# Second FFN planned like the first, unused matmuls at the beginning, other planned durations, norm powers in a stretch of their own

## The chip, the core and the metric

The kernel runs on one core of one Trainium2 chip. Its engines are TensorE (PE, with its weight loads listed apart as PEld), VectorE (DVE), ScalarE (ACT), GpSimd (POOL) and SyncE (SP), which here issues nearly all DMAs. Each engine works through its own queue in order. The metric is the device time of one execution in microseconds (us), the median over several runs. "Clock" is the TensorE clock that was granted, as a share of 2.4 GHz; its lower level is 1.2 GHz.

## The reference

Three steps follow each other: a gated linear attention (4 batches, 8 heads, 768 positions, 48 channels), and two feed-forward networks (FFNs) over 3072 tokens with 384 channels and 2048 hidden ones.

```python
mag = np.sqrt(a_re * a_re + a_im * a_im)
scale = np.minimum(mag, 0.999) / (mag + 1e-06)      # a_re, a_im are multiplied by it
for t in range(S):
    S_re, S_im = ar * S_re - ai * S_im + kv, ar * S_im + ai * S_re
    y[:, :, t] = np.einsum('bhd,bhde->bhe', q[:, :, t], S_re)
# first FFN: silu
h = x @ w_in;  g = h * (1.0 / (1.0 + np.exp(-h)));  x = g @ w_out
# second FFN, beta = 1
h = x @ w_in;  g = np.where(h >= beta, h, np.where(h <= -beta, 0.0, (h + beta) ** 2 / (4.0 * beta)));  out = g @ w_out
```

## The kernel before

**Tiling.** Attention is cut into 12 units (4 batches x 3 blocks of 256 positions). A unit squares a_re and a_im, makes the norm by a logarithm and an exponential (`power` or `window`), scans the decays in blocks (`scan`, nearly all VectorE), forms scaled q and k (`qprime`, `kprime`), transposes them on TensorE with copies by ScalarE (`trans`), and does scores, values and the running state on TensorE (`heads`, `state`). The first FFN goes over 6 pairs of units (512 tokens each) in 16 steps f: nine hidden matmuls into `ph` (`hidden`, L892 to L894), a gate (`gate`: Silu, high part gH, low part gL), and nine output matmuls into three accumulators (L913 to L915). Every product of an FFN is made of three matmuls, because operands are split into a high and a low part. Weights arrive as 64-bit numbers and are converted on VectorE, ScalarE and for some on TensorE (`convert`, 16 tiles for each FFN, k = 0 to 15 and 16 to 31). A tile of the second FFN's weights takes the buffer of one of the first, so its load waits for the last use of that.

**The plan.** `Plan` holds generators. Each yields an engine, a duration and an earliest time for its next operation, or the name of a mark or a ring slot it needs; `go` always takes the operation with the smallest start plus lag and emits it. The durations exist in the plan only: they decide the order of each engine's queue, and the hardware does the rest by semaphores. `lag` ranks the runs: units by their number, weights by `urgent`, the FFN by `behind` (FL = 0.2, or FB = 0.6 while it is ahead of attention).

**What is planned and what isn't.** `first_half` plans attention, the first FFN and all 32 conversions. Then comes a barrier, and the second FFN follows outside the plan, written in program order: `prep` loads one pair's x and splits it (L981, L983), `two` does 16 steps of hidden matmuls, gate (L1011 to L1016) and outputs (L998 to L1000), and the next pair's `prep` is emitted ahead of it. `flag_bad` (a check whether a slow path is needed) is emitted after the second pair.

**Norm powers.** For units 3 to 11 the norm's logarithm and exponential are done in `window` (L217) together with those of the unit before (SEP = 2): two logarithms, then two exponentials.

**Pair 0.** In the first FFN's pair 0 (PEL = 16) gL is made by a matmul with the negative identity (L933) and a copy (L935); in the other pairs by a subtraction on VectorE (L938).

Of the kernel before, what the change touches and what calls it, by code (L numbers as in the profile page):

```python
# [14 lines left out]
PAB = 2  # L15
# [8 lines left out]
class Plan:  # L24
# [6 lines left out]
    def __init__(self):  # L31
        self.free = dict.fromkeys((PE, DVE, ACT, SP, "DMA"), 0.0)
        self.at = {}
        self.runs = []
        self.table = "exp"
        self.log = []
        self.rings = {"t": [2], "pa": [PAB], "ph": [PHB], "gH": [3], "gL": [3], "xq": [1], "sc": [4]}
# [35 lines left out]
    def go(self):  # L73
        while self.runs:
# [30 lines left out]
class Attn:  # L105
# [35 lines left out]
    def loadq(self, i, c):  # L141
        x = self.U[i]["qk"[c]] = self.wp.tile([128, 768], F32, name="qk"[c] + "t")
        t = yield SP, 0.6, 0.0
# [3 lines left out]
    def loadv(self, i):  # L147
        nc, wp, U = self.nc, self.wp, self.U[i]
        U["v"] = []
        for c in range(2):  # L150
            U["v"].append(wp.tile([128, 8, 48], F32, name="vt", bufs=2))
            t = yield SP, 0.5, 0.0
# [88 lines left out]
    def scan(self, i, A, t0=0.0):  # L241
# [81 lines left out]
        if i:  # L323
            yield f"QT{i - 1}"
# [28 lines left out]
    def trans(self, src, nm, t0=0.0):  # L353
# [3 lines left out]
        for g0 in (0, 2):  # L357
# [9 lines left out]
            for g, ps, t1 in pend:  # L367
                t1 = yield ACT, 0.56, t1 + 0.2
# [17 lines left out]
    def knat(self, i):  # L386
        if i < EARLY:
            t0 = yield f"kT{i}"
            self.plan.mark(f"free{i}", t0)
            if i:  # L390
                yield f"st{i - 1}"
# [18 lines left out]
        if i:  # L410
            yield f"st{i - 1}"
# [8 lines left out]
        for c in range(2):  # L420
            kn = wp.tile([128, 8, 96], F32, name="KN", bufs=2)
            t1 = yield SP, 0.8, t2
# [7 lines left out]
    def scores(self, i, QT, KT, c, hh, AT, t0):  # L430
# [4 lines left out]
        t1 = yield PE, 0.95, t0  # L435
# [52 lines left out]
    def heads(self, i, QT, KT, vt, x, t0):  # L488
# [3 lines left out]
        hq, tq = yield "xq", 1  # L492
        xq = wp.tile([128, 2, 256], F32R, name="xq", bufs=1)
        for c in range(2):
            first = u == 0 and c == 0
            sc = []
            for hh in range(2):
                if c:
                    yield f"py{i}"
# [8 lines left out]
            t1 = yield PE, 1.0 + 1.0 * (not first), max(ta, tr, tf)  # L508
# [7 lines left out]
        if u < 2:  # L516
            yield from self.state(i, 1, vt)
        plan.mark(f"st{i}", 0.0)
# [29 lines left out]
    def unit(self, i, x):  # L548
# [36 lines left out]
        tk = yield f"k{i}"  # L585
        t1 = yield from self.kprime(A, U["k"], M[:, 1], r[:, 1], max(t1, tk))
        yield f"QT{i}"
        plan.mark(f"kp{i}", t1)
        if i:
            yield f"h{i - 1}"  # L590
# [4 lines left out]
        xi = yield from x(i)  # L595
        yield from self.heads(i, U["QT"], KT, U["v"], xi, max(t1, tv))

    def ahead(self, i):

        yield f"kp{i - 2}"  # L600
# [6 lines left out]
        t0 = yield f"A{i}"  # L607
# [7 lines left out]
    def queries(self, i, t0):  # L615
# [4 lines left out]
        if i:  # L620
            yield f"h{i - 1}"
# [8 lines left out]
def flag_bad(nc, pool, pp, at, ff):  # L630
    ok = pool.tile([128, 164], F32, name="ok")
    nc.vector.memset(ok, 1.0)
# [4 lines left out]
    low = pool.tile([128, 1], F32, name="low")  # L637
    nc.vector.tensor_reduce(low, ok, mybir.AxisListType.X, ALU.min)
    one = pool.tile([128, 1], F32, name="one")
    nc.vector.memset(one, 1.0)  # L640
    pf = pp.tile([128, 512], F32, name="pf", tag="pa", bufs=PAB)
    nc.tensor.matmul(pf[0:1, 0:1], low, one, start=True, stop=True)
    bad = pool.tile([1, 1], I32, name="bad")
    nc.vector.tensor_scalar(bad, pf[0:1, 0:1], 127.5, None, ALU.is_lt)
    return bad
# [153 lines left out]
class Ffn:  # L799
# [11 lines left out]
    def fetch(self, k):  # L811
        raw = self.wp.tile([128, 1536], I32, name="raw", tag=("wi", "wo")[k % 2] + str(k % 16 // 2))
        t = yield SP, 0.6, 0.0
# [83 lines left out]
    def one(self, n, x, dst):  # L897
        nc, wp, pp, plan = self.nc, self.wp, self.pp, self.plan
        acc = [pp.tile([128, 512], F32, name=f"acc{j}", tag=f"acc{j}") for j in range(3)]
        G = {}  # L900
# [3 lines left out]
        def outs(f):  # L904
            t0 = yield f"g{n}.{f}"
            if n == 0:
                t0 = max(t0, (yield f"w{f // 2 * 2 + 1}"))
            gH, gL, hH, hL = G.pop(f)
# [62 lines left out]
    def prep(self, src):  # L971

        nc, wp = self.nc, self.wp
        raw = wp.tile([128, 3, 512], F32, name="xraw", tag="A", bufs=2)
        x = wp.tile([128, 2, 3, 512], F32R, name="x", bufs=2)
        t = yield SP, 0.6, 0.0
        nc.sync.dma_start(raw, src.rearrange("(j p) t -> p j t", p=128))
        t = self.plan.dma(t, 786)
        for j in range(3):
            t1 = yield ACT, 0.56, t  # L980
            nc.scalar.copy(x[:, 0, j], raw[:, j])  # L981
            yield DVE, 0.61, t1
            nc.vector.tensor_tensor(x[:, 1, j], raw[:, j], x[:, 0, j], ALU.subtract)  # L983
        return x

    def two(self, x, out):
        xH, xL = x[:, 0], x[:, 1]
        nc, tc, wp, pp = self.nc, self.tc, self.wp, self.pp
        acc = [pp.tile([128, 512], F32, name=f"pacc{j}", tag=t, bufs=n)
               for j, (t, n) in enumerate((("acc0", 1), ("acc1", 1), ("acc2", 1), ("pa", PAB)))]  # L990
        pend = []

        def outs(f, gH, gL):
            oH, oL = self.wslices(f, 1)
            for t in range(4):
                s = slice(t * 128, (t + 1) * 128)
                o = acc[t][:, 0:384]
                nc.tensor.matmul(o, gH[:, s], oH, start=f == 0, stop=False)  # L998
# [3 lines left out]
        for f in range(16):  # L1002
            ph = pp.tile([128, 512], F32, name="ph", tag="ph", bufs=PHB)
            for _ in self.hidden(ph, f, xH, xL):
                pass
            c = wp.tile([128, 512], F32, name="c", tag="AT", bufs=2)
            l = wp.tile([128, 512], F32, name="l", tag="KN", bufs=2)
            g = wp.tile([128, 512], F32, name="g", tag="t", bufs=2)
            gH = wp.tile([128, 512], F32R, name="gH", bufs=3)
            gL = wp.tile([128, 512], F32R, name="gL", bufs=3)  # L1010
            nc.vector.tensor_scalar(c, ph, 1.0, -1.0, ALU.min, ALU.max)  # L1011
            nc.scalar.activation(l, ph, AF.Relu, bias=self.cst[:, 0:1])  # L1012
            nc.scalar.activation(c, c, AF.Square, bias=self.cst[:, 1:2], scale=0.5)  # L1013
            nc.vector.tensor_tensor(g, c, l, ALU.add)  # L1014
            nc.scalar.copy(gH, g)  # L1015
            nc.vector.tensor_tensor(gL, g, gH, ALU.subtract)  # L1016
            pend.append((f, gH, gL))
            if len(pend) > 1:
# [212 lines left out]
```

## Time and profile before

| | us |
|---|---|
| median of 3 runs (1159.58 to 1163.02) | 1161.08 |
| the profiled execution | 1160.27 |
| its span | 1158.6 |
| TensorE busy | 1028.6 (89%) |
| VectorE busy | 776.6 (67%) |
| ScalarE busy | 643.2 (56%) |

The span is the time from the first to the last instruction in the profile. Busy time of TensorE counts pipelined matmuls, so a busy TensorE can still run at a low clock: the granted clock has to be read beside it. Averages hide stages with different limits, so the rows below go by stretches: the start (up to 136 us), the first FFN coming in (136 to 204), attention and FFN side by side (204 to 640), the end of the first FFN (640 to 724), the step between the FFNs (724 to 755), and the second FFN (755 to 1128).

### The profile page before, as it was taken

What the parts mean: (1) busy time and instruction counts of PE and PEld (TensorE: products, weight loads), DVE (VectorE), ACT (ScalarE), POOL (GpSimd) and SP (SyncE); (2) the same over time, 40 slices, a digit from 0 to 9 for tenths busy, and PEclk for the clock granted to TensorE, in tenths of its full rate; (3) what the DMA queues carried; (4) which work ended last, traced back from release to release, by engine and by line L of the source; (5) the groups of instructions that cost most, each with busy time, mean ns of one, the idle gap of its engine ahead of it and who ended that gap; (6) DMA issues with size and microseconds to landing.
All of it is one profiled execution on the core that took longest, in us unless ns stands there. A gap on an engine that the chain in (4) does not pass through costs nothing.

```text
span 1158.6 us, 15058 instructions
## 1 busy us (share of the span) xinstructions
PE 1028.6 (89%) x5664; PEld 866.7 (75%) x5664; DVE 776.6 (67%) x1471; ACT 643.2 (56%) x1047; POOL 1.4 (0%) x16
## 2 busy tenths in 40 slices
PE   0374869999999999999999999399999999999997
PEld 0263658677877777787777888289989989989986
DVE  6878889687877877787787278654555355455443
ACT  4454496858385674838566356453555354445443
POOL 0000000000000000000000000000000000000000
PEclk9975879999999999999999999599999999999999
DMA  5402251233131323223221245500101000000000
GB/s 204 171 25 70 75 180 66 73 90 118 28 110 62 97 60 98 88 63 109 63 69 48 72 154 208 193 8 1 56 1 55 1 1 28 1 28 2 28 1 30
DMA packets 47280, 82.06 MB, mean 71 GB/s; under 512 B 24160, under 2 KB 32608, under 8 KB 47200
## 3 DMA queue, kind: packets, MB, share of 16 engines
q1 hardware_dynamic: 47056, 80.92, 21.1%
q8 instruction: 47, 0.77, 0.3%
q14 instruction: 33, 0.27, 0.1%
q10 hardware_dynamic: 144, 0.10, 0.0%
HBM read 61.34 MB, written 17.30 MB: 68 GB/s over the span
## 4 chain that ended last, share of the span: by engine, by line
PE 44%; ACT 4%; DVE 1%; DMA 1%; issue 1%; ACTq 0%; SPq 0%; DVEq 0%
PE ph L892 7%; PE ph L893 7%; PE ph L894 7%; PE pacc L999 6%; PE pacc L998 6%; PE pacc L1000 6%; PE acc L913 1%; PE acc L914 1%; PE acc L915 1%; DMA raw<-in_w_dram 1%; PE py L460 1%; PE psc L438 1%; ACT KT L369 1%; ACT r L217 0%; ACT L217 0%
## 5 line engine op out<-in xcount | busy, mean ns | idle before, releaser
L892 PE MATMUL ph<-x,wi 128*128 128x512 f32 x576 | 232.6, 404 | 17.3 <-ACT x L981 14.6
L893 PE MATMUL ph<-x,wi 128*128 128x512 f32 x576 | 227.8, 396 | 0.5 <-DVE x L983 0.5
L894 PE MATMUL ph<-x,wi 128*128 128x512 f32 x576 | 227.9, 396 | 0.0
L1012 ACT ACTIVATE l<-ph,cst 128x512 f32<-128x512 f32 x96 | 66.2, 689 | 157.0 <-DVE c L1011 157.0
L1011 DVE TENSOR_SCALAR c<-ph 128x512 f32<-128x512 f32 x96 | 66.3, 691 | 118.3 <-PE ph L894 118.2
L892 PEld LDWEIGHTS ph<-x,wi 128*128 128x128 f32 x576 | 109.5, 190 | 42.6 <-ACT x L981 15.3
L998 PE MATMUL pacc<-wo,gH 128*128 128x384 f32 x384 | 129.1, 336 | 1.5 <-ACT gH L1015 1.5
L999 PE MATMUL pacc<-wo,gH 128*128 128x384 f32 x384 | 129.4, 337 | 0.0
L894 PEld LDWEIGHTS ph<-x,wi 128*128 128x128 f32 x576 | 109.1, 189 | 24.3
L893 PEld LDWEIGHTS ph<-x,wi 128*128 128x128 f32 x576 | 109.1, 189 | 21.1 <-DVE x L983 1.2
L1000 PE MATMUL pacc<-wo,gL 128*128 128x384 f32 x384 | 120.0, 336 | 0.0
L914 PE MATMUL acc<-gL,wo 128*128 128x512 f32 x288 | 114.5, 397 | 5.7 <-ACT gL L935 3.0
L913 PE MATMUL acc<-gH,wo 128*128 128x512 f32 x288 | 118.5, 411 | 0.0
L915 PE MATMUL acc<-gH,wo 128*128 128x512 f32 x288 | 114.1, 396 | 0.0
L1014 DVE TENSOR_TENSOR g<-c,l 128x512 f32<-128x512 f32 x96 | 66.1, 688 | 53.5 <-ACT c L1013 53.5
L928 ACT ACTIVATE ph<-ph 128x512 f32<-128x512 f32 x96 | 56.9, 595 | 53.5 <-PE ph L894 52.7
L1016 DVE TENSOR_TENSOR gL<-g,gH 128x512 fp32r<-128x512 f32 x96 | 66.1, 688 | 28.1 <-ACT gH L1015 26.0
L1015 ACT CAST gH<-g 128x512 fp32r<-128x512 f32 x96 | 59.1, 616 | 36.6 <-DVE g L1014 28.7
L938 DVE TENSOR_TENSOR gL<-ph,gH 128x512 fp32r<-128x512 f32 x80 | 54.5, 686 | 31.3 <-ACT gH L930 30.1
L998 PEld LDWEIGHTS pacc<-wo,gH 128*128 128x128 f32 x384 | 72.1, 188 | 4.2 <-ACT gH L1015 1.8
L999 PEld LDWEIGHTS pacc<-wo,gH 128*128 128x128 f32 x384 | 72.1, 188 | 2.7
L1000 PEld LDWEIGHTS pacc<-wo,gL 128*128 128x128 f32 x384 | 71.3, 188 | 0.2
(172 smaller groups left out, 1722.5 us busy)
## 6 DMA issues: line engine op xcount, KB each, us to landing
raw<-in_w_dram SPq DMA_DIRECT2D x32, 768.0 KB, 5.8
A<-in_a_dram SPq DMA_DIRECT2D x12, 768.0 KB, 4.5
kd<-A SPq DMA_DIRECT2D x10, 768.0 KB, 4.0
KN<-kd SPq DMA_DIRECT2D x20, 384.0 KB, 5.5
qt<-in_qk_dram SPq DMA_DIRECT2D x12, 384.0 KB, 3.1
kt<-in_qk_dram SPq DMA_DIRECT2D x12, 384.0 KB, 4.6
vt<-in_vn_dram SPq DMA_DIRECT2D x24, 192.0 KB, 2.5
xd<-x SPq DMA_DIRECT2D x18, 256.0 KB, 2.8
```

What stands on the lines that cost most here:

```text
L892: nc.tensor.matmul(ph, iH[:, j], xH[:, j], start=j == 0, stop=False, skip_group_check=True)
L893: nc.tensor.matmul(ph, iH[:, j], xL[:, j], start=False, stop=False, skip_group_check=True)
L894: nc.tensor.matmul(ph, iL[:, j], xH[:, j], start=False, stop=j == 2, skip_group_check=True)
L913: nc.tensor.matmul(acc[j], oH[:, w], gH, start=f == 0, stop=False)
L914: nc.tensor.matmul(acc[j], oH[:, w], gL, start=False, stop=False)
L915: nc.tensor.matmul(acc[j], oL[:, w], gH, start=False, stop=f == 15)
L998: nc.tensor.matmul(o, gH[:, s], oH, start=f == 0, stop=False)
L999: nc.tensor.matmul(o, gH[:, s], oL, start=False, stop=False)
L1000: nc.tensor.matmul(o, gL[:, s], oH, start=False, stop=f == 15)
L1011: nc.vector.tensor_scalar(c, ph, 1.0, -1.0, ALU.min, ALU.max)
L1012: nc.scalar.activation(l, ph, AF.Relu, bias=self.cst[:, 0:1])
L1014: nc.vector.tensor_tensor(g, c, l, ALU.add)
```

## The change

- The second FFN is planned: `prep` and `two` become generators with marks (`split`, `q`, `o`, `y`), the barrier is gone, and `all_units` adds them to the same plan. Output copies have a lag of -0.5; the last pair stores 128 rows at a time. Outputs of step f are emitted after the hidden matmuls of step f + 2 (DEEP = 2). `flag_bad` is planned too.
- `awake` adds matmuls of 512 columns whose result is not used, from the end of the first scan until the first FFN begins, at a lag of 1.2. Until 16 of them are planned the plan counts TensorE's operations twice (`cold`).
- Durations: copies of `trans` 0.56 to 0.92, scores 0.95 to 0.88, values 1.0 and 2.0 to 0.8 and 1.65. Loads and several steps now carry the time from which they can start. The accumulators of `one` are taken later.
- SEP = 12: every unit's norm powers are done by `power` in `ahead`, and `window` holds two activations only.
- PEL = 0; WE 0.3 to 0.6; FZ = 2.0 is the FFN's lag in pair 0 while it is ahead; the second FFN's weights have a lag of 0.2 in place of 0.3; `kprime` is planned after `qprime`.

```diff
@@ Plan.go
             e, us, t, *more = r[2]
+            if e == PE and self.cold():
+                us *= 2
@@ Attn
-    def loada(self, i):
+    def loada(self, i, t0=0.0):
         A = self.U[i]["A"] = self.wp.tile([128, 1536], F32, name="A", bufs=2)
-        t = yield SP, 0.6, 0.0
+        t = yield SP, 0.6, t0
...
-                t1 = yield ACT, 0.56, t1 + 0.2
+                t1 = yield ACT, 0.92, t1 + 0.2
                 nc.scalar.copy(dv[:, 4 * g:4 * g + 4, :], ps[:96, :].rearrange("p (t x) -> p t x", t=4))
...
-        t1 = yield PE, 0.95, t0
+        t1 = yield PE, 0.88, t0
...
-            t1 = yield PE, 1.0 + 1.0 * (not first), max(ta, tr, tf)
+            t1 = yield PE, 0.8 + 0.85 * (not first), max(ta, tr, tf)
...
         tk = yield f"k{i}"
+        yield f"qp{i}"
         t1 = yield from self.kprime(A, U["k"], M[:, 1], r[:, 1], max(t1, tk))
@@ Ffn
-    def prep(self, src):
+    def prep(self, m, src, xs):
+        t0 = max((yield f"ffn{m}"), (yield f"y{m + PAIRS - 2}"), (yield f"kT{UNITS - 2 + m % 2}"))
+        if m > 1:
+            t0 = max(t0, (yield f"split{m - 2}"))
         raw = wp.tile([128, 3, 512], F32, name="xraw", tag="A", bufs=2)
...
-    def two(self, x, out):
+    def two(self, m, xs, out):
+        tx = yield f"split{m}"
+        x = xs[m]
...
+        def outs(f):
+            t0 = max((yield f"q{m}.{f}"), (yield f"w{16 + f // 2 * 2 + 1}"))
...
+        for f in range(16):
+            tw = yield f"w{16 + f // 2 * 2}"
+            h, tf = yield "ph", 1
+            ph = pp.tile([128, 512], F32, name="ph", tag="ph", bufs=PHB)
+            t1 = yield from self.hidden(ph, f, x[:, 0], x[:, 1], max(tx, tw, tf))
+            if f == 15:
+                plan.mark(f"y{m + PAIRS}", t1)
+            plan.add(0.0, gate(f, ph, h, t1))
+            if f >= DEEP:
+                yield from outs(f - DEEP)
+        for f in range(16 - DEEP, 16):
+            yield from outs(f)
@@ constants
-PEL = 16
+PEL = 0
-SEP = 2
+SEP = 12
+SL = 0.2
+AW = 0.25
-WE = 0.3
+WE = 0.6
+FZ = 2.0
@@ all_units (was first_half)
     def loada(i):
-        yield f"kT{i - 2}"
-        yield f"free{i - 2}"
-        yield from at.loada(i)
+        t = yield f"kT{i - 2}"
+        t = max(t, (yield f"free{i - 2}"))
+        yield from at.loada(i, t)
...
-        return FB if done < 2 * UNITS * 2 and done / 8 - ff.at < TH else FL
+        return (FB if ff.at >= 2 else FZ) if done < 2 * UNITS * 2 and done / 8 - ff.at < TH else FL
...
+    def second_ffn():
+        for m in range(PAIRS):
+            yield f"y{m + PAIRS - 1}"
+            yield from ff.two(m, ys, out[m * 512:(m + 1) * 512, :])
...
+    def awake():
+        t = yield "P0"
+        junk = at.pp.tile([128, 512], F32, name="junk", tag="acc0")
+        while ff.f < 0:
+            t = yield PE, AW, t - 3.0
+            nc.tensor.matmul(junk, at.nid, at.nid.unsqueeze(1).to_broadcast([128, 4, 128]), start=True, stop=True)
+            plan.at["warm"] = plan.at.get("warm", 0) + 1
...
+    plan.cold = lambda: ff.f < 0 and plan.at.get("warm", 0) < 16
...
-            plan.add(0.3, seconds(n))
+            plan.add(SL, seconds(n))
+        for m in range(PAIRS):
+            plan.add(0.5, ff.prep(m, xd2[:, m * 512:(m + 1) * 512], ys))
+        plan.add(FL, second_ffn())
+        plan.add(0.5, flag())
+        plan.add(1.2, awake())
         plan.go()
@@ program
-            first_half(tc, plan, at, ff, xd2)
-            tc.no_sync_barrier()
...
+            all_units(tc, plan, at, ff, xd2, out, fp, bad)
```

## Rows read from the trace of the kernel before

**Rows 1.** Page, totals: busy us (share of the span) xinstructions

```profile
span 1158.6 us, 15058 instructions
PE 1028.6 (89%) x5664; PEld 866.7 (75%) x5664; DVE 776.6 (67%) x1471; ACT 643.2 (56%) x1047; POOL 1.4 (0%) x16
```

**Rows 2.** Stretches: us; PE, PEld, DVE, ACT, POOL busy (xcount); clock; DMA share; GB/s

```profile
37.00:136.00 99.00, 60.27 (x363) 47.25 (x364) 77.72 (x163) 48.95 (x88) 0.00 (x0) 0.74 0.22 80
136.00:204.00 68.00, 58.24 (x318) 47.20 (x318) 60.84 (x111) 53.03 (x88) 0.00 (x0) 0.87 0.39 134
204.00:640.00 436.00, 417.45 (x2522) 336.01 (x2521) 337.53 (x710) 281.32 (x440) 0.00 (x0) 1.00 0.26 79
640.00:724.00 84.00, 83.64 (x435) 68.43 (x433) 52.55 (x73) 43.42 (x80) 0.00 (x0) 1.00 0.42 145
724.00:755.00 31.00, 12.85 (x35) 8.88 (x35) 21.00 (x34) 13.01 (x24) 0.00 (x0) 0.61 0.53 189
755.00:1128.00 373.00, 372.95 (x1877) 338.24 (x1878) 189.19 (x294) 179.05 (x295) 0.00 (x0) 1.00 0.05 16
```

**Rows 3.** TensorE in time, 723 to 755: start, us, engine, instruction, [idle before <-releaser]

```profile
723.25 0.39 PE L915 MATMUL acc<-gH,wo 128*128 128x512 f32 x1
723.48 0.40 PE L913 MATMUL acc<-gH,wo 128*128 128x512 f32 x1
726.55 0.50 PE L914 MATMUL acc<-gL,wo 128*128 128x512 f32 x1 [2.67 <-DVE gL L938]
...
744.34 1.65 PE L892 MATMUL ph<-x,wi 128*128 128x512 f32 x3 [14.56 <-ACT x L981]
```

**Rows 4.** VectorE: groups (busy us, mean ns | idle before, releaser); first conversion in time

```profile
L837 DVE SCALAR_TENSOR_TENSOR raw<-raw 128x768 int32<-128x768 int32 x32 | 30.4, 954 | 0.2
L835 DVE TENSOR_SCALAR raw<-raw 128x768 int32<-128x768 int32 x32 | 17.5, 557 | 10.9 <-DMA raw<-in_w_dram 10.9
L983 DVE TENSOR_TENSOR x<-xraw,x 128x512 fp32r<-128x512 f32 x18 | 11.3, 687 | 0.0
...
668.22 0.56 DVE L835 TENSOR_SCALAR raw<-raw 128x768 int32<-128x768 int32 x1 [0.25 <-DMA raw<-in_w_dram]
```

**Rows 5.** ScalarE: table loads as a group, and one stretch of powers in time

```profile
L217 ACT ACT_TABLE_LOAD x20 | 25.7, 1283 | 0.4
...
574.13 1.28 ACT L217 ACT_TABLE_LOAD   x1
...
581.58 1.07 ACT L928 ACTIVATE ph<-ph 128x512 f32<-128x512 f32 x2
```

**Rows 6.** The beginning in time, on TensorE, ScalarE and VectorE

```profile
52.84 1.16 PE L438 MATMUL psc<-QT,KT 96*128 96x128 f32 x8
60.54 1.91 PE L438 MATMUL psc<-QT,KT 96*128 96x128 f32 x8
135.78 0.50 PE L892 MATMUL ph<-x,wi 128*128 128x512 f32 x1
...
58.32 0.84 ACT L193 ACTIVATE M<-A 128x768 f32<-128x768 f32 x1 [5.53 <-DMA A<-in_a_dram]
...
60.92 0.96 DVE L843 SCALAR_TENSOR_TENSOR raw<-raw 128x768 int32<-128x768 int32 x1 [5.73 <-ACT raw L841]
```

**Rows 7.** TensorE's waits over the run (us, times, longest); the copy group

```profile
PE ptr L365 <- ACT QT L369: 13.5, 16, 2.0
PE psc L438 <- ACT KT L369: 6.2, 9, 1.1
PE pacc L998 <- ACT gH L1015: 1.5, 1, 1.5
...
L369 ACT COPY QT<-ptr 96x512 f32<-96x512 f32 x48 | 48.1, 1079 | 1.0 <-PE ptr L365 1.0
```

**Rows 8.** The two ways to make gL, as groups

```profile
L933 PE MATMUL ph<-gH,nid 128*128 128x512 f32 x16 | 7.3, 469 | 2.8 <-ACT gH L930 2.8
L938 DVE TENSOR_TENSOR gL<-ph,gH 128x512 fp32r<-128x512 f32 x80 | 54.5, 686 | 31.3 <-ACT gH L930 30.1 <-PE acc L914 0.9
```

More of the change, by code (lines that the diff above doesn't have):

```diff
@@ L35, in __init__ @@
         self.table = "exp"
+        self.cold = lambda: False
         self.log = []
@@ L516, in heads @@
         if u < 2:
-            yield from self.state(i, 1, vt)
-        plan.mark(f"st{i}", 0.0)
+            tr = yield from self.state(i, 1, vt)
+        plan.mark(f"st{i}", max(tr, plan.at[f"h{i}"]))
     def state(self, i, c, vt):
@@ L627, in lag, with flag_bad @@
         return lambda: more + LG * (i - sum(f"st{j}" in self.plan.at for j in range(i)))
-def flag_bad(nc, pool, pp, at, ff):
+def flag_bad(nc, pool, pp, at, ff, plan, bad):
     ok = pool.tile([128, 164], F32, name="ok")
+    low = pool.tile([128, 1], F32, name="low")
+    one = pool.tile([128, 1], F32, name="one")
+    yield DVE, 1.0, 0.0
     nc.vector.memset(ok, 1.0)
@@ L636, in flag_bad @@
     nc.vector.tensor_scalar(ok[:96, 68:164], at.mus.rearrange("p i h -> p (i h)"), 1e-14, None, ALU.is_ge)
[L637 removed]
+    t = yield DVE, 0.4, 0.0
     nc.vector.tensor_reduce(low, ok, mybir.AxisListType.X, ALU.min)
[L639 removed]
     nc.vector.memset(one, 1.0)
+    n, tf = yield "pa", 1
     pf = pp.tile([128, 512], F32, name="pf", tag="pa", bufs=PAB)
+    t = yield PE, 0.2, max(t + 1.0, tf)
     nc.tensor.matmul(pf[0:1, 0:1], low, one, start=True, stop=True)
[L643 removed]
+    t = yield DVE, 0.1, t + 1.0
     nc.vector.tensor_scalar(bad, pf[0:1, 0:1], 127.5, None, ALU.is_lt)
[L645 removed]
+    plan.drop("pa", n, t)
 def slow_attention(nc, tc, q, k, v, a_re, a_im, xd):
@@ L898, in one @@
         nc, wp, pp, plan = self.nc, self.wp, self.pp, self.plan
-        acc = [pp.tile([128, 512], F32, name=f"acc{j}", tag=f"acc{j}") for j in range(3)]
-        G = {}
+        G, acc = {}, []
         tx = max((yield f"x{2 * n}"), (yield f"x{2 * n + 1}"))
@@ L907, in outs @@
                 t0 = max(t0, (yield f"w{f // 2 * 2 + 1}"))
+            if f == 0:
+                acc.extend(pp.tile([128, 512], F32, name=f"acc{j}", tag=f"acc{j}") for j in range(3))
             gH, gL, hH, hL = G.pop(f)
@@ L1000, in outs, with gate @@
                 nc.tensor.matmul(o, gL[:, s], oH, start=False, stop=f == 15)
[L1002 to L1005, printed above, removed]
+                if f == 15:
+                    plan.add(0.0, store(t, t1))
+            plan.drop("gH", hH, t1)
+            plan.drop("gL", hL, t1)
+        def gate(f, ph, h, t1):
+            hH, tH = yield "gH", 1
+            gH = wp.tile([128, 512], F32R, name="gH", bufs=3)
+            hL, tL = yield "gL", 1
+            gL = wp.tile([128, 512], F32R, name="gL", bufs=3)
@@ L1016, in two @@
             nc.vector.tensor_tensor(gL, g, gH, ALU.subtract)
-            pend.append((f, gH, gL))
-            if len(pend) > 1:
-                outs(*pend.pop(0))
-        for x in pend:
-            outs(*x)
-        for u in range(2):
-            o = wp.tile([128, 2, 384], F32, name="o", tag=("qt", "kt")[u])
-            nc.vector.tensor_copy(o[:, 0], acc[2 * u][:, 0:384])
-            nc.scalar.copy(o[:, 1], acc[2 * u + 1][:, 0:384])
-            nc.sync.dma_start(out[u * 256:(u + 1) * 256, :].rearrange("(t p) d -> p t d", p=128), o)
+            plan.drop("t", ht, t1)
@@ L1029 @@
+        for f in range(16 - DEEP, 16):
+            yield from outs(f)
+        plan.mark(f"two{m}", 0.0)
 WN = 4
-PEL = 16
+PEL = 0
 DEEP = 2
@@ L1155, in program @@
             xd2 = dp.tile([384, 3072], F32, name="xd2")
-            first_half(tc, plan, at, ff, xd2)
-            tc.no_sync_barrier()
-            def prep(m):
-                return drain(ff.prep(xd2[:, m * 512:(m + 1) * 512]))
-            x = prep(0)
-            for m in range(6):
-                nx = prep(m + 1) if m < 5 else None
-                ff.two(x, out[m * 512:(m + 1) * 512, :])
-                if m == 1:
-                    bad = flag_bad(nc, fp, pp, at, ff)
-                x = nx
+            bad = fp.tile([1, 1], I32, name="bad")
+            all_units(tc, plan, at, ff, xd2, out, fp, bad)
         rv = nc.values_load(bad, min_val=0, max_val=1)
@@ L1174, in program @@
                 slow_ffn(nc, tc, w1i, w1o, w2i, w2o, xd, out)
-def drain(gen):
-    try:
-        next(gen)
-        while True:
-            gen.send(0.0)
-    except StopIteration as stop:
-        return stop.value
 _INS = ['q', 'k', 'v', 'a_re', 'a_im', 'moe_w_in', 'moe_w_out', 'moe2_w_in', 'moe2_w_out']
```

136 lines of the change are left out of this document (88 added, 48 removed).

## The prediction

> **What bounds the kernel now.** I read the page's totals first, then a table of six stretches, then who TensorE waited for, and last the instruction lists of the places where it stood. TensorE is busy 1028.6 of 1158.6 us [rows 1], so the question is where the other 130 us are and where its clock is low. The table of stretches [rows 2] answers that. From 755 to 1128 (the second FFN) TensorE is busy 372.95 of 373.00 at clock 1.00, and from 640 to 724 (end of the first FFN) 83.64 of 84: nothing but less matmul work helps there. From 204 to 640 (attention units beside FFN pairs) it is busy 417.45 of 436, so 18.5 us are idle. From 724 to 755, between the two FFNs, it issues 35 matmuls in 31 us at a mean clock of 0.61. From 37 to 136 it is busy 60.27 of 99 at 0.74, while VectorE is busy 77.72: there VectorE's chain of scans sets the pace and TensorE is cold and waiting. From 136 to 204 TensorE is busy 58.24 of 68 at 0.87, and VectorE 60.84. TensorE is thus the bound from about 160 us on; before that it is VectorE's chain, with what that waits for.
>
> The reader should see that after 160 us every microsecond in which TensorE neither idles nor runs slow shortens the span by itself, and that before it only what lies on the way to the first FFN matmul (at 135.78 us [rows 6]) counts.
>
> **Part 1, the second FFN in the same plan.** Today the order of the first half is written out, then come all remaining weight conversions, and only then the load and split of x. So the first hidden matmul of the second FFN waits 14.56 us for the split on ScalarE [rows 3], after a stop of 2.67 us within the first FFN's last outputs. At full clock 512-column matmuls follow each other every 0.23 us (723.25 and 723.48 [rows 3]). The 35 matmuls of 724 to 755 are then 35 x 0.23 = 8 us of work; 31 - 8 = 23 us are lost there.
>
> After the change x of pair 0 is loaded as soon as its buffer (that of pair 4 of the first FFN) is free, well before the first FFN ends, and the hidden matmuls of the second FFN may follow the last hidden ones of the first. They need only the first weights, whose conversion starts at 668 [rows 4]. What hides the conversions is that the weights for step f are wanted only some 4 us x f later. The cover is thin on VectorE: a conversion is one operation of 0.557 us and three of 0.954 (the row of one stands for all three) [rows 4], so 3.42 us, and 16 of them are 54.7 us; the splits of two x are 6 x 0.687 = 4.1 [rows 4]; about 13 subtractions for gL at 0.686 are 9 [rows 8]; and the second FFN's own gates take half of VectorE (189.19 of 373 [rows 2]), from 724 to 755 some 15.7 us. The sum is 83.5 us of work in the 87 us from 668 to 755. It fits, but queued gates will wait behind conversions. I leave 2 us of the 23 lost: **-21**, with bounds -23 and -13 (10 us kept, about three conversions late).
>
> Beyond the boundary the second FFN's matmuls stay as many, and there is no idle to win (372.95 of 373). Each pair now ends with its own last outputs before the next pair's hidden matmuls are issued; two output groups of 12 matmuls lie between a gate and its use, which is enough by the end of today's kernel, where only 1.5 us is waited for gH [rows 7]. I take 0 for the pairs and **-1** for the end, since DEEP is 2 there and the last rows are stored in smaller pieces (0 to -2). The flag's operations move into the plan; one matmul of one column costs nothing beside this.
>
> **Part 2, the beginning.** Three things. First, loads are now planned from the time at which their buffer is free. The row to see is ScalarE's square of unit 2, which stands 5.53 us at the head of its queue for the load of A, and VectorE then waits 5.73 us for what is queued behind it [rows 6]. With the load's true start in the plan the square is placed later: -5.7, if nothing else is late next; next is the score matmul, and that is the second thing.
>
> Second, unused matmuls keep TensorE running from the end of the first scan until the first hidden matmul. Eight score matmuls take 1.16 us at 52.84, right behind transposes and weight matmuls, and 1.91 us at 60.54, after TensorE had stood while ScalarE waited for A [rows 6]: 0.75 us for each such group. TensorE's 60.27 us at clock 0.74 would be 60.27 x 0.74 = 44.6 at full clock, so 15.7 us are lost to the low clock. VectorE's 21.3 idle us (99 - 77.72) less the 5.7 above bound what of it can lie on the path: 0 to 15.6. VectorE is the nearer limit for most of the chain, so I take a third: -5.
>
> Third, PEL = 0: in pair 0 the low part gL is made on VectorE, not by a matmul on TensorE with a copy on ScalarE. It removes 16 matmuls of 0.23 us (3.7 us of TensorE) with 2.8 us of waits before them, and adds 16 x 0.686 = 11 us to VectorE [rows 8], which has 68 - 60.84 = 7.2 us free in 136 to 204 [rows 2]. The two cancel within -4 to +4; I take 0 net. The larger lag of FFN work in pair 0 gives attention its turn first and costs TensorE nothing that is not work already queued. Together **-10** for the beginning; bounds -20, and above zero only by the first rival below.
>
> **Part 3, other durations and the norm powers.** In 204 to 640 TensorE stands 18.5 us. Over the whole run the largest heads of queues are transposes waiting for the QT copies (13.5 us in 16 times) and scores waiting for the KT copies (6.2 us) [rows 7]. A copy takes 1.079 us [rows 7]; the plan had 0.56 and now has 0.92, so TensorE's order will put FFN matmuls where it now stands. I expect half of the 11 us that these two cost in this stretch. Against it: the norm powers of units 3 to 11 leave the combined stretch. A stretch of logarithms and exponentials is framed by three table loads of 1.283 us [rows 5] (before the logarithms, before the exponentials, before the next Silu). Nine more stretches are at most 27 loads, 34.6 us of ScalarE, which goes from 281.3 of 436 [rows 2] to about 316. It is not the bound, and a single block becomes shorter: today's is 581.58 - 574.13 = 7.45 us [rows 5], and a new one has the same three loads but two activations fewer. I take 1.5 us off the gain: **-4**, bounds -10 and +17 (half of the 34.6 us reaching TensorE).
>
> The rows show a logarithm and an exponential loading a table each, with the next activation right behind the load. The Trainium skill, "ScalarE: Activation LUTs", section "Table sets: the hidden batching unit", says to batch activations by table set, and has both functions in one set; this change does the opposite of batching, and this trace shows two loads where the page would have one. Its section "What ACT_TABLE_LOAD costs" adds about 1.38 us of drain to each load; an estimate by that page doubles the price to about 72 us of ScalarE and the sum to some 20 us worse, but no row here shows that drain.
>
> **The sum.** -21 - 1 - 10 - 4 = -36. The profiled run took 1160.27 us with a span of 1158.6, so 1124.3; the median of the runs is 0.8 above that run: 1125.
>
> **The rivals.**
>
> *Slower: unused matmuls at half clock.* They are planned at 0.25 us. In 37 to 136 there are 99 - 44.6 = 54 us to fill, some 216 of them. If the clock stayed at its lower level they would take 2 x 0.23 = 0.46 us each, 45 us more, in front of the transposes and scores in an in-order queue: 1125 + 10 + 45 = 1180. It ends slower than before from about three quarters of that stretch at half clock. Against it: TensorE at 96% busy keeps 1.00 over 204 to 640 [rows 2]. Chance 0.07.
>
> *The powers in a stretch of their own hold up the gates.* ScalarE's extra blocks let Silu come late, and TensorE waits at the hidden or output matmuls: +17 in place of -4, 1146. For it: the plan counts one table load where two happen. Against: in 204 to 640 no wait for Silu or gL stands among TensorE's large waits. Chance 0.13. (The batching rule of the Trainium skill's page "ScalarE: Activation LUTs" would lead to this case too.)
>
> *The boundary isn't closed.* VectorE's 83.5 of 87 us turn into waits of the second FFN's first steps: 8 us of the gain go, 1133; the matmuls stand in the same place, only shorter. Chance 0.15. The change would then not do all that it says.
>
> *The beginning gives more.* If all of VectorE's idle in 37 to 136 goes (21 us, where I take 10): 1114. Chance 0.13.
>
> **How the numbers follow.** My forecast has 0.52; predicted 1125 us. Its own range is 1114 to 1137. With the rivals the range is 1107 to 1148: the low end is -23 - 20 - 8 - 2, the high end the second rival; 0.8 within. About 0.3% is what a measurement can tell from no change. Faster by more: 0.88; within: 0.04 (the second and the third rival together with nothing won at the beginning, 1146 + 8 + 10 = 1164); slower: 0.08 (the first rival, and 0.01 for what I haven't thought of).
>
> **What would show it.** In the profile after: a stretch around 690 to 750 with TensorE at 1.00 and hardly a wait between last outputs of the first FFN and first hidden matmuls of the second; the first hidden matmul near 125 in place of 135.78; a granted clock near 1.00 from 45 us on; no ScalarE wait of several us for A; up to 27 more table loads; less idle than 18.5 us in the middle. I am wrong if the first hidden matmul comes later than 136, if VectorE's queue holds the second FFN's first pair, or if TensorE's waits in the middle name Silu.

## The result and the profile after

| | before | after |
|---|---|---|
| median | 1161.42 us | 1109.93 us (1107.7 to 1111.18) |
| span of the profiled execution | 1158.6 us | 1105.9 us |

The median before is that of the three runs shown above and one more. The ratio is 0.9555 (95% interval 0.9534 to 0.9576). Forecast were 1125 us and 36 us less; measured are 51.5 us less.

The page's totals after, answering [rows 1]:

```profile
span 1105.9 us, 15082 instructions
PE 1022.3 (92%) x5718; PEld 868.0 (78%) x5718; DVE 792.8 (72%) x1487; ACT 687.5 (62%) x1057; POOL 1.4 (0%) x16
```

TensorE is busy for nearly as long as before (1022.3 us, 70 unused matmuls included, against 1028.6); most of the 52.7 us of span came out of its idle time. The table of stretches after, answering [rows 2] (columns as there), with one stretch more, 240 to 640:

```profile
37.00:136.00 99.00, 73.66 (x474) 56.92 (x475) 94.36 (x188) 66.69 (x114) 0.00 (x0) 0.92 0.32 116
136.00:204.00 68.00, 60.43 (x333) 48.23 (x331) 64.90 (x123) 50.02 (x83) 0.00 (x0) 0.97 0.27 90
204.00:640.00 436.00, 428.96 (x2668) 356.36 (x2669) 337.77 (x713) 310.92 (x456) 0.00 (x0) 0.99 0.29 87
240.00:640.00 400.00, 397.41 (x2452) 329.70 (x2452) 310.16 (x643) 284.79 (x418) 0.00 (x0) 1.00 0.28 85
640.00:724.00 84.00, 81.67 (x374) 68.76 (x373) 72.42 (x98) 57.84 (x98) 0.00 (x0) 1.00 0.42 155
724.00:755.00 31.00, 31.00 (x159) 28.25 (x158) 15.32 (x23) 15.06 (x23) 0.00 (x0) 1.00 0.00 1
755.00:1080.00 325.00, 322.15 (x1606) 288.65 (x1605) 171.62 (x260) 164.67 (x251) 0.00 (x0) 1.00 0.06 20
```

Read the fourth column of numbers (VectorE) in the first row: 94.36 of 99 us, where it was 77.72. In 204 to 640 TensorE is idle for 7.0 us, where it was 18.5, and the hole at 724 to 755 is gone. But from 755 on TensorE is no longer without a gap: 2.85 of 325 us idle, where it was 0.05 of 373.

The span is best cut at two instructions of TensorE that both kernels have:

| | before | after | difference | forecast |
|---|---|---|---|---|
| first hidden matmul of the first FFN | 135.8 | 114.4 | -21.4 | -10 |
| from there to the last output matmul of the first FFN | 593.4 | 574.3 | -19.1 | -4 - 2.7 |
| from there to the end of the span | 429.4 | 417.2 | -12.2 | -22 + 2.7 |

(The 2.7 us are the stop within the first FFN's last outputs [rows 3], which the prediction counted with the boundary.) The total was off by 17 us of span, made of -11, -12 and +7: two errors add up, and the third hides 7 us of them.

### The profile page after: what moved, and what is told of

Same layout as the page of the kernel before. It is cut to its first block, busy times and chain, and to the rows that moved or that the text cites. A ratio compares the mean times of both kernels' runs of the same rounds, so it can differ in the third digit from the quotient of the medians.

```text
span 1105.9 us, 15082 instructions
## 1 busy us (share of the span) xinstructions
PE 1022.3 (92%) x5718; PEld 868.0 (78%) x5718; DVE 792.8 (72%) x1487; ACT 687.5 (62%) x1057; POOL 1.4 (0%) x16
## 4 chain that ended last, share of the span: by engine, by line
PE 78%; DVE 9%; ACT 4%; issue 1%; DMA 0%; SPq 0%; ACTq 0%; DVEq 0%
PE ph L900 10%; PE ph L902 10%; PE ph L901 10%; PE pacc L1045 6%; PE pacc L1043 6%; PE pacc L1044 6%; PE acc L922 5%; PE acc L923 5%; PE acc L924 5%; PE psc L440 4%; PE py L462 3%; PE ptr L368 3%; PE pS L533 2%; DVE raw L845 1%; DVE room L851 1%
## 5 line engine op out<-in xcount | busy, mean ns | idle before, releaser
L1045 PE MATMUL pacc<-wo,gL 128*128 128x384 f32 x384 | 130.9, 341 | 3.5 <-DVE gL L1072 3.5
L922 PE MATMUL acc<-gH,wo 128*128 128x512 f32 x288 | 118.6, 412 | 0.0
L1066 ACT ACTIVATE c<-c,cst 128x512 f32<-128x512 f32 x96 | 69.5, 724 | 65.5 <-DVE c L1063 65.5
L947 DVE TENSOR_TENSOR gL<-ph,gH 128x512 fp32r<-128x512 f32 x96 | 65.2, 685 | 27.0 <-ACT gH L939 26.5
L1043 PEld LDWEIGHTS pacc<-wo,gH 128*128 128x128 f32 x384 | 72.2, 188 | 6.1 <-ACT gH L1070 2.6
```

What stands on the lines that cost most here:

```text
L922: nc.tensor.matmul(acc[j], oH[:, w], gH, start=f == 0, stop=False)
```

## The experiments

All were timed against the kernel before on the same chip. "Cost" is (ratio - 0.955) x 1162 us: what the kernel loses against the changed one; by the intervals it is uncertain by 3 to 5 us. "Idle" is TensorE's in 240 to 640, 400 us less the busy time in the windows of each trace. The other columns are the first and second line of the table above, from the one profiled execution of each run. The kernel before has 135.8, 593.4 and an idle time of 14.5 there.

| run | edit to the changed kernel | ratio, 95% interval | cost | first hidden | to end of FFN 1 | idle |
|---|---|---|---|---|---|---|
| e0_after_again | none | 0.9549 (0.9527 to 0.9572) | 0 | 114.6 | 574.3 | 2.6 |
| e1_no_unused | no unused matmuls | 0.9739 (0.9705 to 0.9773) | 22 | 125.2 | 589.6 | 12.5 |
| e2_old_loads | loads planned from 0 | 0.9708 (0.9674 to 0.9743) | 18 | 126.7 | 587.7 | 9.4 |
| e9_neither | both of these | 0.9654 (0.9630 to 0.9678) | 12 | 126.2 | 574.7 | 3.8 |
| e3_powers_back | SEP = 2 | 0.9747 (0.9718 to 0.9777) | 23 | 116.8 | 596.1 | 14.5 |
| e5_gl_on_pe | PEL = 16 | 0.9670 (0.9642 to 0.9697) | 14 | 118.6 | 586.2 | 12.3 |
| e7_lag_fb | FZ = 0.6 | 0.9734 (0.9709 to 0.9758) | 21 | 118.2 | 595.1 | 15.9 |
| e6_copy_056 | copy planned at 0.56 | 0.9820 (0.9796 to 0.9845) | 31 | 121.2 | 600.4 | 21.5 |
| e14_copy_091 | copy planned at 0.91 | 0.9684 (0.9658 to 0.9710) | 16 | 117.6 | 587.0 | 10.4 |
| e16_copy_093 | copy planned at 0.93 | 0.9573 (0.9551 to 0.9595) | 3 | 120.0 | 575.7 | 4.5 |
| e8_ffn2_apart | second FFN as before | 0.9630 (0.9597 to 0.9664) | 9 | 117.4 | 574.7 | 4.0 |
| e4_only_ffn2 | second FFN planned, all else as before | 0.9850 (0.9805 to 0.9895) | 35 | 134.3 | 596.7 | 15.9 |

**The boundary: with and without the planned second FFN.** e8_ffn2_apart takes the second FFN out of the changed kernel's plan again, e4_only_ffn2 puts it into the old one.

In e8_ffn2_apart the old `prep`, `two`, `flag_bad`, the barrier and the loop over the pairs are back:

```diff
-        for m in range(PAIRS):
-            plan.add(0.5, ff.prep(m, xd2[:, m * 512:(m + 1) * 512], ys))
-        plan.add(FL, second_ffn())
-        plan.add(0.5, flag())
...
+            tc.no_sync_barrier()
...
```

In e4_only_ffn2 the constants, durations, loads and earliest times of the old kernel are back, without unused matmuls (two small steps stay: the later accumulators of `one`, and `kprime` behind `qprime`):

```diff
-SEP = 12
+SEP = 2
-PEL = 0
+PEL = 16
-        plan.add(1.2, awake())
...
```

> The changed kernel with the second FFN outside the plan and behind the barrier, as before; all other parts of the change stay. Theory, that the parts add: 1110 + 22 = about 1132 us, with the first hidden matmul of the first FFN at 114.4 as in the changed kernel and a stop of 14 to 15 us before the second FFN. Rival, that the boundary's gain and the rest overlap: 1122 us or less, or 1140 and more.

> Only part 1 of the change: the second FFN in the plan; everything else as before (durations, loads, norm powers, gL on TensorE in pair 0, lags, no unused matmuls). Theory, that the parts add and the boundary is worth 21 us and the end 1: about 1139 us, first hidden matmul near 135.8. Rival, that the boundary closes only with the first half's other order: 1148 us or more.

Measured: 1121.29 and 1146.89 us; by the ratios the planned second FFN is worth some 9 us in the changed kernel and 17 in the old one (0.9850; its interval reaches the 22 of the sum). The stretch itself tells more: from the first FFN's last output to the end of the span it is 427.2 us in e8_ffn2_apart against 417.2 after (10.0), and 415.7 in e4_only_ffn2 against 429.4 before (13.7), less than the forecast both times. The hole itself is closed as forecast. TensorE's waits of e8_ffn2_apart (us in all, times, longest) have it again:

```profile
PE ph L896 <- ACT x L986: 13.5, 1, 13.5
```

and TensorE in time after (columns as in [rows 3]) goes from the first FFN's last output to the second one's hidden matmuls in 0.23 us, and then stops elsewhere:

```profile
688.66 0.39 PE L924 MATMUL acc<-gH,wo 128*128 128x512 f32 x1
688.89 0.39 PE L900 MATMUL ph<-x,wi 128*128 128x512 f32 x1
...
697.01 0.44 PE L1043 MATMUL pacc<-wo,gH 128*128 128x384 f32 x1 [1.67 <-ACT gH L1070]
...
697.29 0.33 PE L1044 MATMUL pacc<-wo,gH 128*128 128x384 f32 x1
698.28 0.44 PE L1045 MATMUL pacc<-wo,gL 128*128 128x384 f32 x1 [0.66 <-DVE gL L1072]
```

VectorE and ScalarE in time at that place show what the first gate of the second FFN waited behind. Its `g` is done at 694.2, but its copy gH starts only at 696.35.

```profile
693.51 0.69 DVE L1068 TENSOR_TENSOR g<-c,l 128x512 f32<-128x512 f32 x1 [0.38 <-ACT c L1066]
...
694.84 0.72 ACT L1066 ACTIVATE c<-c,cst 128x512 f32<-128x512 f32 x1 [0.79 <-DVE c L1063]
...
695.47 0.89 ACT L849 ACTIVATE T<-raw 128x768 f32<-128x768 f32 x1
...
696.35 1.13 ACT L1070 CAST gH<-g 128x512 fp32r<-128x512 f32 x2
696.67 0.95 DVE L851 SCALAR_TENSOR_TENSOR T<-T,raw 128x768 int32<-128x768 int32 x1
...
697.54 1.28 DVE L1072 TENSOR_TENSOR gL<-g,gH 128x512 fp32r<-128x512 f32 x2
```

In ScalarE's queue the next gate's square (L1066), which waits 0.79 us for VectorE, and one operation of a conversion (L849, 0.89 us) stand ahead of gH; then a conversion's operation on VectorE (L851) stands ahead of gL. So the conversions are a part of the two stops, and the order of the gates' own operations is the other.

TensorE's waits in the whole second FFN after:

```profile
PE pacc L1045 <- DVE gL L1072: 3.5, 5, 0.8
PE pacc L1043 <- ACT gH L1070: 1.7, 1, 1.7
```

That is 5.2 us, where before there were 2.6 (1.5 for gH [rows 7], 0.6 and 0.5 at the first hidden matmuls). Two of them are the stops just shown; the other four come once for each pair, 68.2 us apart (766, 835, 903, 971). The first of these, with what VectorE did ahead of it:

```profile
765.15 0.68 DVE L995 TENSOR_TENSOR x<-xraw,x 128x512 fp32r<-128x512 f32 x1
765.18 0.34 PE L1043 MATMUL pacc<-wo,gH 128*128 128x384 f32 x1
...
765.75 0.69 DVE L1072 TENSOR_TENSOR gL<-g,gH 128x512 fp32r<-128x512 f32 x1
...
766.49 0.44 PE L1045 MATMUL pacc<-wo,gL 128*128 128x384 f32 x1 [0.79 <-DVE gL L1072]
```

It is the first output group of a pair, which has only three hidden groups ahead of it, and a split of x is queued before its gL. The last pair, with no further x to split, has no such stop. This is the part that I had taken as 0, and it is larger than its waits. The first hidden matmul of pair 1 and that of pair 5, before and then after, enclose the same number of matmuls (1346 records):

```profile
813.38 0.40 PE L892 MATMUL ph<-x,wi 128*128 128x512 f32 x1
...
1080.81 0.40 PE L892 MATMUL ph<-x,wi 128*128 128x512 f32 x1
```
```profile
758.88 0.40 PE L900 MATMUL ph<-x,wi 128*128 128x512 f32 x1
...
1031.71 0.40 PE L900 MATMUL ph<-x,wi 128*128 128x512 f32 x1
```

That is 267.4 us before and 272.8 after: the planned pairs are 5.4 us slower. With the second FFN outside the plan (e8_ffn2_apart) it is 267.4 again, and with it alone planned (e4_only_ffn2) 272.8. The trace of the kernel before shows why it had no such stops. Its second FFN does not stand in TensorE's queue in the order of the program text: it lies outside the block `manual_schedule`, five hidden groups (45 matmuls, 744.34 to 759.09) come ahead of the first output, and later hidden matmuls stand between an output's gH and gL matmuls. The planned order gives that up. Whether a plan with more hidden groups ahead would win the 5 us back was not tried.

**The beginning, its two steps one by one and together.** e1_no_unused leaves out the unused matmuls and the doubled TensorE durations that go with them; e2_old_loads plans every load from time 0 again; e9_neither does both.

```diff
# e1_no_unused, e9_neither
-    plan.cold = lambda: ff.f < 0 and plan.at.get("warm", 0) < 16
-        plan.add(1.2, awake())
# e2_old_loads, e9_neither
-        yield from at.loada(i, t)
+        yield from at.loada(i)
...
-        raw = yield from ff.fetch(16 + k, t)
+        raw = yield from ff.fetch(16 + k)
```

> The changed kernel without the unused matmuls (and without counting TensorE's first operations twice). Theory, that the low clock lay on the way to the first FFN matmul: the granted clock of 37 to 136 us falls from 0.92 to about 0.75, VectorE is idle there some 10 us more than the 4.6 us of the changed kernel, the first hidden matmul moves from 114.4 to about 124, and the time is about 1120 us. Rival, that only the start times of the loads gave the beginning its gain: the clock falls, but the first hidden matmul stays within 3 us of 114.4 and the time within 1109 to 1113 us.

> The changed kernel with all loads planned from time zero again, as before; the unused matmuls stay. Theory: ScalarE stands some 5 us at the head of its queue for A of unit 2 again, VectorE behind it, the first hidden matmul comes 5 to 8 us later than 114.4, and the time is about 1116 us. Rival, that a warm TensorE alone took the 21 us off the beginning: the wait returns but its 5 us are absorbed; time within 1109 to 1113 us.

> The changed kernel with both steps of the beginning undone: no unused matmuls (and no doubled TensorE durations in the plan), and loads planned from time 0 again. Undone one by one they cost 21 and 18 us. Theory one (they are one gain: both serve VectorE's chain, and the rest of each was the middle's order): both together cost little more than one, 1130 to 1138. Theory two (two gains that add up): 39 us, 1149. By the prediction's beginning step the two together are worth 10.7 us: 1121.

Measured: 1134.19, 1130.82 and 1121.89 us. Undoing both is cheaper than undoing either. The first hidden matmul is at 125.2, 126.7 and 126.2, so all three lose 11 to 12 us at the beginning: the two steps bring it forward only together. (The nine kernels with both start between 114.4 and 121.2, so part of the 12 us can be the order's.) The rows say what each is for. The unused matmuls keep the clock up: in 80 to 114 us it is 1.00 after and 0.54 in e1_no_unused. VectorE's waits for TensorE's score matmuls in 37 to 136 (us, times, longest), first after, then e1_no_unused:

```profile
DVE AT L446 <- PE psc L440: 0.6, 2, 0.4
```
```profile
DVE AT L446 <- PE psc L440: 7.4, 6, 1.5
```

and ScalarE in time in e2_old_loads, where a square stands at the head of its queue for A again, twice (after has no such wait in this stretch):

```profile
57.15 0.84 ACT L196 ACTIVATE M<-A 128x768 f32<-128x768 f32 x1 [2.97 <-DMA A<-in_a_dram]
...
103.45 0.84 ACT L196 ACTIVATE M<-A 128x768 f32<-128x768 f32 x1 [2.91 <-DMA A<-in_a_dram]
```

What e1_no_unused and e2_old_loads lose beyond that, some 13 to 15 us, is lost after the first hidden matmul: 589.6 and 587.7 us to the end of the first FFN, where e9_neither needs 574.7, as the changed kernel does. The two stretches of e9_neither:

```profile
37.00:136.00 99.00, 64.14 (x380) 50.77 (x381) 83.81 (x171) 55.98 (x96) 0.00 (x0) 0.88 0.30 103
240.00:640.00 400.00, 396.25 (x2491) 329.58 (x2490) 312.80 (x664) 291.67 (x427) 0.00 (x0) 1.00 0.28 84
```

So with an equal middle the two steps are worth 12 us; as e1_no_unused and e2_old_loads alone would have it, they were worth 40. In all runs VectorE waits for the scores 4.5 to 7.4 us in this stretch without the unused matmuls and 0.6 to 2.3 with them.

**The other steps, undone one by one.** The edits are one constant each.

```diff
# e3_powers_back
-SEP = 12
+SEP = 2
# e5_gl_on_pe
-PEL = 0
+PEL = 16
# e7_lag_fb
-FZ = 2.0
+FZ = 0.6
# e6_copy_056
-                t1 = yield ACT, 0.92, t1 + 0.2
+                t1 = yield ACT, 0.56, t1 + 0.2
```

> The changed kernel itself, on the chip of the next three runs, so that each of them can be set against it. Expected: 0.9555 of the kernel before, as in the first measurement (0.9534 to 0.9576), with the first hidden matmul at 114.4 us.

> The changed kernel with the norm powers of units 3 to 11 in the combined stretch again (SEP = 2 in place of 12). What it tells: whether 26 more table loads cost anything. Theory: ScalarE is not the bound (310.9 of 436 us busy in 204 to 640), so the loads are hidden; within 2 us of the changed kernel's 1109.9, by the prediction's step 1.5 us faster, 1108.4. Rival one (table loads reach TensorE): 17 us faster, about 1093. Rival two: a combined block of about 7.5 us makes Silu or the QT copies late, where a single block does not; 5 to 8 us slower, about 1116, with PE's waits for ACT QT back above 10 us.

> The changed kernel with the low part gL of pair 0 made by TensorE and ScalarE again (PEL = 16 in place of 0). What it tells: which engine is short in 114 to 204 us. Prediction's step: 3.7 us of TensorE and 2.8 us of waits against 11 us of VectorE cancel; 1109.9, within 4. Theory now (VectorE still sets the pace after the first hidden matmul: it is 94.4 of 99 us busy in 37 to 136 and TensorE waits 10.3 us for VectorE's gL in pair 0): 11 us come off VectorE and these waits go, 4 to 9 us faster, 1101 to 1106. Rival: TensorE and ScalarE are the ones that are short, 4 us slower, 1114.

> The changed kernel with the first FFN's lag in pair 0 as in all others (FZ = 0.6 in place of 2.0). Prediction's step: the larger lag costs TensorE nothing and wins nothing by itself; within 2 us of 1109.9. Rival: without it FFN matmuls of pair 0 go in front of transposes and scores of the first units, so VectorE's chain, which is the limit there, gets its work later: 6 to 10 us slower, 1116 to 1120, with the first hidden matmul earlier than 114.4 us.

> The changed kernel with the planned duration of the QT and KT copies at 0.56 us again, in place of 0.92; on the chip a copy takes 1.08 us either way. Prediction's step: 5.5 us of TensorE's waits for these copies come back, 1115, with PE's waits for ACT QT and KT from 5.0 to above 10 us. Rival (order of the pairs): waits for the copies are a small part; the loss is at the starts of pairs, 8 to 20 us, 1118 to 1130. What tells them apart is the sum of TensorE's waits for ACT QT and ACT KT against its idle time and clock in 340 to 350, 440 to 450 and 540 to 550.

Measured: 1110.06 for the changed kernel itself; 1133.6, 1125.48, 1132.19 and 1141.11 us for the four. Each of the four lost more than any theory gave it, and the losses look alike: little at the first hidden matmul (2 to 7 us), most of it in the middle. With e1 and e2 the single costs come to about 130 us (22 + 18 + 23 + 14 + 21 + 31), where the whole change brought 51.5. They can't all be prices of the steps.

**An edit that means nothing.** To see how much of this is the order alone, I changed the planned duration of the copies by a hundredth of a microsecond, up and down.

```diff
-                t1 = yield ACT, 0.92, t1 + 0.2
+                t1 = yield ACT, 0.91, t1 + 0.2      # e16_copy_093: 0.93
```

> The changed kernel with the planned duration of the QT and KT copies at 0.91 us in place of 0.92: a hundredth of a microsecond in the plan, nothing on the chip. It reorders TensorE's queue from about 60 us on all the same, since the plan always takes the smallest start. What it tells: how much of what single steps cost (15 to 24 us each, when one was undone) is the step itself, and how much is that the order falls out differently. Theory one (each step has its own price): no change, 1110, within 3. Theory two (what counts is whether the first FFN comes to the end of a pair before attention has the next x; any reordering can bring that back): 8 to 20 us slower, 1118 to 1130, with TensorE idle and at a clock below 1.00 near 340 to 350, 440 to 450 and 540 to 550, where the changed kernel has neither.

> The changed kernel with the planned copy at 0.93 us in place of 0.92, the other neighbour of e14_copy_091 (0.91), which cost 15.5 us. What it tells: whether the changed kernel's order is one among equals or an unusually good one. Theory one (its 1110 is the usual outcome and 0.91 an unlucky order): 1110, within 4. Theory two (an order without stops at the starts of pairs is the exception): 1118 to 1130, again with TensorE idle for 8 us or more in 240 to 640, where the changed kernel has 2.6.

Measured: 1125.5 and 1114.33 us. At 0.91 the kernel loses 16 us for nothing, with the same picture as the others: 3 us at the first hidden matmul, 13 us after it. The stretches of e14_copy_091:

```profile
240.00:640.00 400.00, 389.62 (x2402) 322.20 (x2403) 303.13 (x637) 277.03 (x404) 0.00 (x0) 0.98 0.27 80
440.00:460.00 20.00, 16.22 (x74) 12.90 (x75) 17.12 (x24) 16.64 (x22) 0.00 (x0) 0.91 0.54 158
540.00:560.00 20.00, 17.18 (x99) 13.95 (x99) 17.05 (x28) 15.93 (x22) 0.00 (x0) 0.91 0.45 139
```

TensorE is idle 10.4 us in the middle, against 2.6. Its clock is below 1.00 in three stretches of 20 us: 240 to 260 (0.83; after has 0.93 there) and the two shown, which lie 100 us apart, at the same point of two pairs. At 340 to 360, where the expectation had put another, it is 1.00 with 1.0 us idle. One of these places in time, on TensorE:

```profile
543.00 0.64 PE L368 MATMUL ptr<-ident,Q 128*96 128x128 f32 x4 [2.10 <-ACT QT L372]
544.36 1.00 PE L368 MATMUL ptr<-ident,Q 128*96 128x128 f32 x4 [0.72 <-ACT QT L372]
545.02 0.78 PE L900 MATMUL ph<-x,wi 128*128 128x512 f32 x1
545.59 0.63 PE L901 MATMUL ph<-x,wi 128*128 128x512 f32 x1
546.02 0.63 PE L902 MATMUL ph<-x,wi 128*128 128x512 f32 x1
```

Attention's transposes stand in the queue ahead of FFN matmuls and wait for copies; then the FFN matmuls follow each other every 0.43 us for some 3 us, in place of 0.23, at the lower clock. e7_lag_fb has the other kind of it at 349: a pair's first hidden matmul waits for x itself, which attention has just finished.

```profile
345.51 0.32 PE L304 MATMUL pe<-ident,X 48*128 48x48 f32 x2 [1.69 <-ACT X L299]
348.93 0.77 PE L900 MATMUL ph<-x,wi 128*128 128x512 f32 x1 [3.10 <-DMA x<-xq]
349.50 0.63 PE L901 MATMUL ph<-x,wi 128*128 128x512 f32 x1
```

The kernels fall into two groups: those with an idle time of 4.5 us or less in the middle need 574 to 576 us to the end of the first FFN (the changed kernel, e8, e9, e16), all others 586 to 600, the kernel before among them. Which group a kernel lands in can change with a hundredth of a microsecond in the plan. So a single undone step whose loss lies in the middle and is not above the 16 us of e14_copy_091 (e5_gl_on_pe) says nothing of the step. Of a larger one (e1, e2, e3, e7) at most the excess could be the step's, and two neighbours are a small sample: another order may cost more than 16 us. e6_copy_056, at 31 us, has a mark of its own. Its waits of TensorE for the copies over the run:

```profile
PE ptr L368 <- ACT QT L372: 10.0, 20, 1.1
PE psc L440 <- ACT KT L372: 5.8, 9, 1.1
```

against those after:

```profile
PE ptr L368 <- ACT QT L372: 3.4, 4, 2.1
PE psc L440 <- ACT KT L372: 1.6, 2, 1.2
```

The first line of each is no mark: e1_no_unused, with 0.92, waits 12.7 us for QT copies. The second is: the scores wait 5.8 to 6.2 us in 9 times for KT copies in the three kernels that plan 0.56 (before, e4, e6), and 1.3 to 2.2 us in 2 to 4 times in all others. So some 4 of the 31 us are shown to be the step's; how the rest divides between it and the order, no run separates.

## Why the prediction was right, and where its terms were off

**Sign, size and range** held (1107 to 1148; its low end takes -8 for the middle, where that term's own bound is -10); the forecast's own range (1114 to 1137) didn't, and the error lies in three terms.

**The boundary, -21 and the pairs 0.** The hole of 14.56 us is gone. The cover on VectorE held and was less thin than worked out: the conversions run from 631.5 to 719.5, and VectorE is busy 73.89 of these 88 us, where the sum had 83.5 of 87. The stops in the second FFN's first output group cost 1.67 + 0.66 us, near the 2 that were left for them, though only a part of them is conversions. The step that failed is "I take 0 for the pairs": they cost 5.4 us. Two output groups lie between a gate and its use in the middle of a pair, as I argued, but none at its beginning; and that today's kernel hardly waits was no evidence for it, since its queue has another order. The end of the span gave little: the last output matmul is 7.1 us ahead of it after and 7.3 before. In all, 12.2 of the forecast 19.3 us came in this stretch, and the pairs are most of what is missing. The stop of 2.67 us [rows 3] didn't belong to the boundary at all: e4_only_ffn2 still has it (2.65 us), and e8_ffn2_apart, without the planned second FFN, has not. The rival "the boundary isn't closed" described the place rightly (the first steps of the second FFN), at a third of its price.

**The beginning, -10.** Its two priced steps, loads and unused matmuls (-10.7 together), measured 12 (e9_neither), less what the order may have in it. Priced apart, at -5.7 and -5, they were wrong: neither shows a gain alone. Of the mechanism for the unused matmuls, VectorE's wait for the scores was right (7.4 to 0.6 us); the count was not: 70 of them ran, not some 216. They have a lag of 1.2, so the plan puts other work first. The other 9.6 us of the -21.4 come from what I had priced at 0: e9_neither has neither step and starts at 126.2, e4_only_ffn2 with all the rest as before at 134.3. Which of the remaining steps it is, stays open; undone one by one they move the start by 2 to 7 us, and the meaningless edits by 3 and 6. VectorE's row says what the 21.4 us are: from 37 us to the first hidden matmul it is busy 77.7 of 98.8 us before and 73.0 of 77.4 after, so 16.7 us are idle time and 4.7 us are work that now comes later. The fourth rival, "the beginning gives more" (-21, all of VectorE's idle time), has the mechanism for the larger part; that its number fits so well is luck.

**"TensorE is the bound from about 160 us on"** put the limit too early. In 136 to 204 VectorE is busy 64.90 of 68 us after, and TensorE waits for it: with gL of pair 0 made on VectorE (PEL = 0) 10.3 us of waits for gL stand in 110 to 204.

```profile
PE acc L923 <- DVE gL L947: 10.3, 3, 4.5
```

In e5_gl_on_pe these are gone, and 3.4 us for gH come in their place; but its middle is one of the long ones, so whether PEL = 0 gains or loses is not settled by it.

**The middle, -4.** The step on the copies was right in kind and half in size: of the 11.4 us that transposes and scores waited for copies in 204 to 640, 0.8 is left, where I kept half. What the sum had no term for is the order itself: e14_copy_091 is the same work and 13 us slower in this stretch. So the same steps give 19.1 us here with one order and 6.4 with another; without the stop of 2.67 us, -16.4 lies outside the bounds (-10 to +17). With the order of e14_copy_091 the change would have given 1125.5 us, where the forecast was: that the result is better is in part the luck of an order. No run reorders the kernel before in the same way, so how far its own middle (593.4 us) is an unlucky order stays open.

**The norm powers' table loads.** The groups of loads after, answering [rows 5]:

```profile
L937 ACT ACT_TABLE_LOAD x21 | 26.9, 1283 | 0.4
L220 ACT ACT_TABLE_LOAD x20 | 25.7, 1283 | 0.4
L208 ACT ACT_TABLE_LOAD x8 | 10.3, 1283 | 0.1
L210 ACT ACT_TABLE_LOAD x8 | 10.3, 1283 | 0.1
```

With one more at the start they are 58 loads, 26 more than before, as forecast (up to 27), and ScalarE is busy 310.92 us in 204 to 640 (forecast 316). No wait for Silu showed up among TensorE's. The rule of the Trainium skill, "ScalarE: Activation LUTs", section "Table sets: the hidden batching unit", would have made e3_powers_back, which batches again, the faster one. It was 23 us slower with 26 loads fewer; how much of that is the order, no run separates. So the 26 loads (33 us of ScalarE) cost nothing that a row shows, and what batching would give at an equal order is not shown.

**The first rival**, unused matmuls at half clock, did not happen: the clock in 37 to 136 rose from 0.74 to 0.92, and it is 1.00 from 55 to 115 us.

None of the eleven edited kernels was faster than the changed one; e16_copy_093 came next.

## What to carry over

Where a greedy plan writes the order, an edit has two effects, its own and that of a new order, and the second can be the larger. Before a step is priced by undoing it, change something that can't matter and see what that costs; and compare the pieces (time to a named instruction, idle time by stretch) and not totals, since a step's own price shows in its place while the order's shows elsewhere. Steps that serve the same chain should be undone together as well as apart.

## What the runs showed that was not expected

**Two engines that read one PSUM tile.** The plan starts ScalarE's `l` and VectorE's `c` of a gate side by side. In the traces the one that is emitted second waits for the first, in either order; whether the chip asks for that or only the semaphores of the program, no run shows. VectorE's largest wait in the second FFN after, then ScalarE's before, each with its count:

```profile
DVE c L1063 <- ACT l L1061: 60.6, 84, 4.2
```
```profile
ACT l L1012 <- DVE c L1011: 157.0, 88, 7.4
```

The plan counts them as parallel, so its gates are planned shorter than they are.

**The clock after a short stop.** The stops of 2.10 and 0.72 us at 543 in e14_copy_091 were followed by some 3 us at the lower clock (0.43 us between 512-column matmuls, where it is 0.23 at the higher), after a long stretch at full clock; the stops of 1.67 and 0.66 us at 697 in the changed kernel were not (clock 1.00 in 690 to 700). A stop of TensorE can so cost more than the time it stands.
